# One wait each for the exponentials and the maxima, with eight fixed probability buffers

## The chip, the cores and the metric

The kernel runs on one core of one Trainium2 chip. The metric is device time in microseconds (us) of one execution, as the median of several runs. In the text PE is TensorE (matmuls; PEld are its weight loads), DVE is VectorE, ACT is ScalarE, POOL is GpSimd and SP is SyncE, which issues nearly all transfers. Each engine works through its own queue in order, and engines wait for each other by semaphores.

## The reference

Two attention blocks read the same input x of 2048 rows and 448 columns, with 16 heads of 28 columns each. Block A looks at eight keys per row (itself and every second row back), block B at all 2048. A gate per row mixes them:

```python
g = _sigmoid((x * gate_w).sum(-1, keepdims=True))
a = _A_ref(x, A_wqkv, A_wo)      # eight keys per row, dilation 2
b = _B_ref(x, B_wqkv, B_wo)      # full softmax attention
return g * a + (1 - g) * b

# inside _B_ref
scores = jnp.einsum("bhqd,bhkd->bhqk", q, k) * (Dh ** -0.5)
p = _softmax(scores, axis=-1)
o = jnp.einsum("bhqk,bhkd->bhqd", p, v)
```

## The kernel before

**Precision.** Float32 operands of the projections and the scores are split into a high part that the fast matmul format holds and a low part with the rest; three products (high with high, high with low, low with high) replace one.

**Stages.** From 0 to about 255 us the kernel projects x to q, k and v (lines 290 and 295), and computes the first row maxima on the side (lines 142 and 159). From about 255 to 840 us it runs the loop on which the change bears. After that come the last output projection and stores.

**The loop.** It has 16 units (a group of four heads by a block of 512 queries), each of 16 steps (128 keys), so 256 steps. In one step, `scores` issues on PE twelve score matmuls (line 955: four heads, three split products each), and between them up to three matmuls of another kind, s0, s1 and s2 (line 142): scores for the row maxima of a later unit. DVE reduces those to maxima (line 146), s0 alone and s1 with s2 as a pair. ACT takes the exponentials of the four heads as two instructions of two heads each (line 958). PE ends the step with eight matmul records that multiply the previous step's probabilities by V (line 921, called av). The maxima enter as two more rows of the contraction, so that the exponential needs no bias. In the last 20 steps all maxima are done, and s0 to s2 are left out.

**Its PSUM tiles.** Three tiles of two banks go round. One of them, called `one` in `scores` (T2 in the profile's buffer numbers), takes heads "1" and "2" in every step with s matmuls. The other two, `mine` and `other`, change places from step to step: `mine` takes heads "3" and "0", and `other` takes s1 and s2. So the pair of maxima that DVE takes from `other` must be done before PE may write head "3" of the next step there, and the second exponential of a step must be done before PE may write s1 and s2 of the next step. s0 has a bank of its own, T1.

**What sets the order.** The scheduling is by hand: each engine executes in the order of the code. A planner in the same file deals the work of block A (products on POOL, reductions on DVE, an exponential on ACT) to the steps. The semaphore waits are derived from the tiles that each instruction reads and writes. An instruction carries one wait itself; more waits become instructions of their own (EVENT_SEMAPHORE) ahead of it in the same queue.

**Probabilities.** Every exponential asks a pool of eight buffers for a new tile, `pair("P")`.

Of the kernel before, what the change touches and what calls it, by code (L numbers as in the profile page):

```python
# [10 lines left out]
AF = mybir.ActivationFunctionType  # L11
ALU = mybir.AluOpType
X = mybir.AxisListType.X
# [6 lines left out]
SCALE = DH ** -0.5  # L20
NU = NG * NB
NMX = 192
# [3 lines left out]
def gated_mix_kernel(ctx: ExitStack, tc: tile.TileContext, xT, xn, gw, wA, wB, woAB, out):  # L26
    nc = tc.nc
# [45 lines left out]
    MX = cp.tile([128, NMX], F32, name="MX")  # L73
# [10 lines left out]
    def pair(name):  # L84
        return pp.tile([128, 2, 512], F32, tag="P", name=name)
# [50 lines left out]
    def s1_mm(n, bank, half=False):  # L136
        u, i = divmod(n, 64)
        qs, kc, h = i // 16, i // 4 % 4, i % 4
        if i == 0 and u + 1 < NU:
            load_qhi(u + 1)  # L140
        r = slice(64 * (h // 2), 64 * (h // 2) + 64) if half else slice(32 * h, 32 * h + DH)
        nc.tensor.matmul(bank, qhis[u][h % 2][r, 128 * qs:128 * qs + 128],  # L142
                         KH[u // NB % 3][r, 512 * kc:512 * kc + 512], start=True, stop=True)

    def s1_max(n, k, bank):
        nc.vector.tensor_reduce(MX[:, n % NMX:n % NMX + k], bank, axis=X, op=ALU.max)  # L146
        if n // 64 != (n + k) // 64:
            finished.append(n // 64)
        s1c[0] = n + k
# [53 lines left out]
    with tc.tile_pool(name="xp", bufs=1) as xp, tc.tile_pool(name="wp", bufs=2) as wp:  # L203
# [208 lines left out]
        for kt in range(3):  # L412
            if kt < 2:
                nc.vector.tensor_copy(xh[0][:, kt, :], r[:, kt, :])
            nc.vector.tensor_tensor(out=xl[0][:, kt, :], in0=r[:, kt, :], in1=xh[0][:, kt, :].bitcast(F32),
                                    op=ALU.subtract)
        nc.vector.tensor_tensor(out=tail[64:128], in0=t[64:128], in1=tail[64:128].bitcast(F32), op=ALU.subtract)
        nc.vector.tensor_tensor(out=wl0[:, 3, 0:256], in0=wt0[:, 0:256], in1=wh0[:, 3, 0:256].bitcast(F32),
                                op=ALU.subtract)
# [27 lines left out]
        for n, t in enumerate(tiles):  # L447
# [4 lines left out]
            for w in splits:  # L452
                i, k = (n - splits[w][0]) * splits[w][1], splits[w][1]
# [42 lines left out]
            if n == 64:  # L496
                gate = []
                for sgn, dst in ((-1.0, g_t), (1.0, omg)):
                    e = sp.tile([128, NJ], F32, name="ez")
# [174 lines left out]
    for c in range(8):  # L674
# [20 lines left out]
        n = 0  # L695
# [236 lines left out]
    def scores(u, kt, cur):  # L932
        g = u // NB
        n = s1c[0]
        k = min(3, s1e - n)
        qh, ql = Qs[u]
        ks = slice(128 * kt, 128 * kt + 128)
        one, mine, other = ring
        ring[:] = (one, other, mine) if k else (other, one, mine)
        bank = {"1": one[:, 0, :], "2": one[:, 1, :], "3": mine[:, 0, :], "0": mine[:, 1, :],  # L940
                "s0": T1, "s1": other[:, 0, :], "s2": other[:, 1, :]}
        for tok in WITH if k else ALONE:
            if tok[0] == "s":
                i = int(tok[1])
                if i < k:
                    s1_mm(n + i, bank[tok])
                if i == 0:
                    s1_max(n, 1, T1)
                elif i == 2 and k > 1:
                    s1_max(n + 1, k - 1, other[:, 0:k - 1, :])  # L950
                continue
            a, t = tok[0], int(tok[1])
            h = (int(a) + n) % 4
            r = slice(32 * h, 32 * h + (DH + 2 if t == 0 else DH))
            nc.tensor.matmul(bank[a], (KH[g % 3], KH[g % 3], KL[g % 2])[t][r, ks], (qh, ql, qh)[t][r, :], start=(t == 0), stop=(t == 2))  # L955
            if t == 2 and a in "20":
                p = pair("P")
                nc.scalar.activation(p, one if a == "2" else mine, AF.Exp, scale=SCALE)  # L958
                cur[(h + 3) % 4], cur[h] = p[:, 0, :], p[:, 1, :]
                yield len(cur)  # L960

    for u in range(NU):
        g, b = divmod(u, NB)
        for kt in range(NJ):
# [12 lines left out]
            for a in scores(u, kt, cur):  # L977
                if a == 2:
                    run("mid", st)
# [66 lines left out]
```

## Time and profile before

| what | value |
|---|---|
| median of 3 runs | 921.59 us (920.6 to 921.7) |
| the profiled execution | 921.93 us |
| its span, first to last instruction | 920.1 us |
| busy: PE, DVE, ACT, POOL | 99%, 79%, 71%, 70% |
| granted clock of PE | 0.999 |
| from 255 to 800 us: DVE, ACT, POOL busy | 494, 478 and 484 of 545 us |

A profile's group of instructions is read as: line, engine, operation, what it writes and reads, shapes, count; then busy time in us and mean ns of one; then the idle time of the engine just before them and what ended it. In a timeline each row is a start in us, a duration in us, and the instruction; the time in brackets is the engine's idle time before it and what ended that. The chain of work lists, in order of time, what the end of the execution hung on; "issue" there is time in which nothing that the profile shows was waited for. An "ACTq" or "DVEq" belongs to the engine's queue, not to its arithmetic.

### The profile page before, as it was taken

How to read it: one execution, taken by the hardware profiler on the slowest of the kernel's cores; microseconds unless marked ns; L12 is line 12 of the kernel's file. 1: busy time of each engine (PE TensorE's matmuls, PEld its weight loads, DVE VectorE, ACT ScalarE, POOL GpSimd, SP SyncE). 2: the span in 40 equal slices, each digit the busy share in tenths (PEclk: the TensorE clock that was granted, in tenths of full speed). 3: DMA queues.
4: the chain of work that ended last, by engine and by line, in shares of the span. 5: the costliest groups of instructions: out<-in, count | busy, mean ns of one | idle time of the engine just before them, and what ended most of it. 6: DMA issues, size and time to landing. Idle time of an engine off the chain costs nothing.

```text
span 920.1 us, 21384 instructions
## 1 busy us (share of the span) xinstructions
PE 912.2 (99%) x8390; PEld 546.5 (59%) x8390; DVE 728.8 (79%) x934; ACT 650.0 (71%) x797; POOL 640.6 (70%) x505
## 2 busy tenths in 40 slices
PE   9999999999999999999999999999999999999998
PEld 6799999999944444444444444444444444335997
DVE  5588999998979999999999999999999988511221
ACT  6456434343388888888888888888888888996221
POOL 2489846464468649999899999999898996800100
PEclk9999999999999999999999999999999999999999
DMA  9877402558363341225235315421411322353772
GB/s 260 288 242 198 152 12 82 148 129 113 96 241 84 88 115 45 83 62 131 60 77 148 81 45 141 98 96 36 107 37 33 91 55 43 86 172 85 205 218 88
DMA packets 103966, 105.11 MB, mean 114 GB/s; under 512 B 64136, under 2 KB 73736, under 8 KB 103080
## 3 DMA queue, kind: packets, MB, share of 16 engines
q1 hardware_dynamic: 103720, 103.47, 41.3%
q8 instruction: 66, 1.08, 0.5%
q10 hardware_dynamic: 144, 0.26, 0.1%
q14 instruction: 36, 0.29, 0.1%
HBM read 62.72 MB, written 40.96 MB: 113 GB/s over the span
## 4 chain that ended last, share of the span: by engine, by line
PE 95%; DMA 3%; SPq 1%; ACT 1%; POOL 0%; DVE 0%; issue 0%; ACTq 0%
PE T L955 31%; PE av L921 28%; PE r L295 15%; PE T L804 7%; PE r L290 4%; PE r L142 4%; PE T L142 4%; DMA V<-in_xT 1%; DMA qk_hi<-qkh 1%; PE T L782 1%; DMA KH<-qk_hi 0%; SPq L217 0%; ACT P L958 0%; POOL wl L212 0%; DMA QP<-qk_hi 0%; ACT raw L358 0%
## 5 line engine op out<-in xcount | busy, mean ns | idle before, releaser
L958 ACT ACTIVATE P<-T 128x1024 f32<-128x1024 f32 x512 | 497.4, 1026 | 67.0 <-PE T L955 66.0
L146 DVE TENSOR_REDUCE MX<-T 128x1 f32<-128x512 f32 x470 | 448.9, 955 | 45.2 <-PE T L955 17.8
L921 PE MATMUL av<-P,V 128*32 128x512 f32 x2048 | 272.7, 605 | 0.9 <-ACT osb L822 0.9
L955 PEld LDWEIGHTS T<-QH,KH 30*128 30x128 f32 x1024 | 92.9, 181 | 238.3 <-ACT P L958 198.6
L142 PE MATMUL T<-KH,QP 28*128 28x512 f32 x704 | 225.0, 470 | 0.1
L955 PE MATMUL T<-QH,KH 30*128 30x512 f32 x1024 | 223.2, 493 | 0.2
L159 DVE TENSOR_REDUCE MX<-r 128x2 f32<-128x1024 f32 x160 | 192.1, 1222 | 25.6 <-PE r L142 22.3
L955 PE MATMUL T<-QL,KH 28*128 28x512 f32 x1024 | 191.9, 394 | 0.0
L955 PE MATMUL T<-QH,KL 28*128 28x512 f32 x1024 | 191.7, 391 | 0.0
L599 POOL TENSOR_TENSOR prod<-qt,kt 128x896 f32<-128x896 f32 x64 | 135.3, 2114 | 8.5 <-DMA kt<-a_scr 5.2
L358 ACT ACTIVATE raw<-r 128x896 f32<-128x896 f32 (+1 forms) x64 | 58.9, 921 | 97.9 <-PE r L295 94.6
L654 POOL TENSOR_TENSOR oat<-oat,prod 128x896 f32<-128x896 f32 x56 | 118.2, 2111 | 2.7
L142 PEld LDWEIGHTS T<-KH,QP 28*128 28x128 f32 x704 | 86.0, 181 | 24.7 <-ACT P L958 9.9
L359 POOL TENSOR_TENSOR ast<-raw 128x448 f32<-128x448 f32 x48 | 55.5, 1155 | 58.8 <-ACT raw L358 49.0
L649 POOL TENSOR_TENSOR prod<-vt,L 128x896 f32<-128x896 f32 x56 | 95.5, 1706 | 0.4
L955 PEld LDWEIGHTS T<-QH,KL 28*128 28x128 f32 x1024 | 93.6, 182 | 0.9
L955 PEld LDWEIGHTS T<-QL,KH 28*128 28x128 f32 x1024 | 93.6, 184 | 0.0
L921 PEld LDWEIGHTS av<-P,V 128*32 128x32 f32 x2048 | 40.3, 108 | 80.8 <-issue 67.6
L295 PE MATMUL r<-wh,xh 64*128 64x448 f32 (+1 forms) x512 | 82.9, 363 | 0.1
L142 PE MATMUL r<-KH,QP 64*128 64x512 f32 x320 | 80.6, 393 | 0.6 <-DVE MX L159 0.4
L295 PE MATMUL r<-wh,xl 64*128 64x448 f32 (+1 forms) x384 | 70.4, 364 | 0.0
L604 POOL TENSOR_TENSOR prod<-prod 128x448 f32<-128x448 f32 x64 | 65.6, 1026 | 5.0
(109 smaller groups left out, 1072.8 us busy)
## 6 DMA issues: line engine op xcount, KB each, us to landing
a_scr<-ast SPq DMA_DIRECT2D x24, 448.0 KB
qk_hi<-qkh SPq DMA_DIRECT2D x24, 256.0 KB
qk_lo<-qkh SPq DMA_DIRECT2D x24, 256.0 KB
rbc<-rs SPq DMA_DIRECT2D x64, 64.0 KB
QP<-qk_hi SPq DMA_DIRECT2D x64, 56.0 KB
KL<-qk_lo SPq DMA_DIRECT2D x16, 224.0 KB
QH<-qk_hi SPq DMA_DIRECT2D x64, 56.0 KB
QL<-qk_lo SPq DMA_DIRECT2D x64, 56.0 KB
```

The costliest lines, as they stand in the source:

```text
L142: nc.tensor.matmul(bank, qhis[u][h % 2][r, 128 * qs:128 * qs + 128], KH[u // NB % 3][r, 512 * kc:512 * kc + 512], start=True, stop=True)
L146: nc.vector.tensor_reduce(MX[:, n % NMX:n % NMX + k], bank, axis=X, op=ALU.max)
L159: nc.vector.tensor_reduce(m, PM[k], axis=X, op=ALU.max)
L295: nc.tensor.matmul(bank[:, 0:cols], x, ws[c][rows, k, 0:cols], start=first, stop=last)
L599: nc.gpsimd.tensor_tensor(out=p, in0=qt[c], in1=kvt["k", c % 2][:, HALO - DIL * w:HALO - DIL * w + NJ, :], op=ALU.mult)
L604: nc.gpsimd.tensor_tensor(out=lo, in0=lo, in1=hi, op=ALU.add)
L649: nc.gpsimd.tensor_tensor(out=dst.rearrange("p j (h d) -> p j h d", d=DH), in0=kvt["v", c % 2][:, HALO - DIL * w:HALO - DIL * w + NJ, :].r ...
L654: nc.gpsimd.tensor_tensor(out=oat[c], in0=oat[c], in1=oat[c, w], op=ALU.add)
L804: writes(bank, nc.tensor.matmul(bank[:, :D], src, wo[c][k], start=(first and k == ks[0] and i == 0), stop=(last and k == ks[-1] and i == 2)))
L921: nc.tensor.matmul(av[32 * h:32 * h + 32, :], V[:, kt, 4 * g + h, :], tiles_[h], start=(kt == 0), stop=(kt == NJ - 1), skip_group_check=True)
L955: nc.tensor.matmul(bank[a], (KH[g % 3], KH[g % 3], KL[g % 2])[t][r, ks], (qh, ql, qh)[t][r, :], start=(t == 0), stop=(t == 2))
L958: nc.scalar.activation(p, one if a == "2" else mine, AF.Exp, scale=SCALE)
```

## The change

The first eight exponentials take the eight buffers of the pool, and from then on each takes the buffer of the one eight before it, without asking the pool. Three kinds of dependence are declared absent: of an exponential on the exponential eight before it (both are ACT's, and PE's reading lies between), of an exponential on the last four pairs or singles of maxima, and of a maximum on the last eight exponentials. In each case the code's reason is that the wait for PE that stays behind implies the one that goes.

```diff
+    exps, maxs, probs = [], [], []
+
     def s1_max(n, k, bank):
-        nc.vector.tensor_reduce(MX[:, n % NMX:n % NMX + k], bank, axis=X, op=ALU.max)
+        i = nc.vector.tensor_reduce(MX[:, n % NMX:n % NMX + k], bank, axis=X, op=ALU.max)
+        for e in exps[-8:]:
+            tc.declare_no_dep(i.ins, e, reason="PE waited for it and the maximum waits for PE")
+        maxs.append(i.ins)
...
             if t == 2 and a in "20":
-                p = pair("P")
-                nc.scalar.activation(p, one if a == "2" else mine, AF.Exp, scale=SCALE)
+                if len(exps) < 8:
+                    probs.append(pair("P"))
+                p = probs[len(exps) % 8]
+                e = nc.scalar.activation(p, one if a == "2" else mine, AF.Exp, scale=SCALE).ins
+                for o in exps[-8:-7]:
+                    tc.declare_no_dep(e, o, query=mybir.DependencyQuery.ANY_SYNC,
+                                      reason="PE has read what it wrote, and this one waits for PE")
+                for o in maxs[-4:]:
+                    tc.declare_no_dep(e, o, reason="PE waited for it and the exponential waits for PE")
+                exps.append(e)
```

No instruction of arithmetic and no transfer changes its place on any engine. What changes is the list of waits. In ACT's queue the exponentials of the loop stood with two waits each; this is a stretch of the second unit before, behind the copy of the first unit's result (T_3270 is the tile `one`, the other two are `mine` in turn; PE_49, DVE_49, Activation_49 and DMAHW1_49 are the semaphores of PE, DVE, ACT itself and a transfer queue):

```order
L822 ACTIVATE osb<-av 128x512 [waits DMAHW1_49,PE_49]
L958 ACTIVATE P<-T_3270 128x1024 [waits PE_49,Activation_49]
L958 ACTIVATE P<-T_3266 128x1024 [waits DVE_49,PE_49]
L958 ACTIVATE P<-T_3270 128x1024 [waits PE_49,Activation_49]
L958 ACTIVATE P<-T_3262 128x1024 [waits DVE_49,PE_49]
```

The same stretch of ACT's queue with the change:

```order
L827 ACTIVATE osb<-av 128x512 [waits DMAHW1_49,PE_49,Activation_49]
L965 ACTIVATE P<-T_3270 128x1024 [waits PE_49]
L965 ACTIVATE P<-T_3266 128x1024 [waits PE_49]
L965 ACTIVATE P<-T_3270 128x1024 [waits PE_49]
L965 ACTIVATE P<-T_3262 128x1024 [waits PE_49]
```

In the whole program 277 exponentials lose a wait for ACT's own semaphore, which stood on the exponential itself while a separate instruction ahead held the wait for PE. Another 223 lose a wait for DVE, which was the separate instruction while the exponential held the wait for PE. 14 of the copies of line 822 (827 in the changed file) gain a wait for ACT's own semaphore, and their wait for PE moves to the separate instruction. ACT's queue has 197 instructions that only wait, against 694.

In DVE's queue the pairs of maxima (128x2) had two waits and the singles (128x1) one, here in the middle of the loop:

```order
L146 TENSOR_REDUCE MX<-T_3274 128x1 [waits PE_49]
L146 TENSOR_REDUCE MX<-T_3262 128x2 [waits PE_49,Activation_49]
L146 TENSOR_REDUCE MX<-T_3274 128x1 [waits PE_49]
L146 TENSOR_REDUCE MX<-T_3266 128x2 [waits PE_49,Activation_49]
L609 TENSOR_REDUCE L<-prod 128x16 [waits Pool_49]
```

The same place with the change:

```order
L148 TENSOR_REDUCE MX<-T_3274 128x1 [waits PE_49]
L148 TENSOR_REDUCE MX<-T_3262 128x2 [waits PE_49]
L148 TENSOR_REDUCE MX<-T_3274 128x1 [waits PE_49]
L148 TENSOR_REDUCE MX<-T_3266 128x2 [waits PE_49]
L614 TENSOR_REDUCE L<-prod 128x16 [waits Pool_49]
```

Here 233 pairs lose the wait for ACT, and with it the separate instruction that held the wait for PE. PE's, POOL's and SP's queues hold the same waits as before, for the same counts.

## Prediction

> **What bounds the kernel now.** The page comes first, for where time can be won at all, then the busy times of the three parts of the run.
>
> ```profile
> PE 912.2 (99%) x8390; PEld 546.5 (59%) x8390; DVE 728.8 (79%) x934; ACT 650.0 (71%) x797; POOL 640.6 (70%) x505
> ...
> 255.00:800.00 545.00, 544.67 (x5463) 224.09 (x5461) 494.18 (x676) 478.00 (x536) 483.88 (x344) 1.00 0.32 87
> 800.00:840.00 40.00, 39.09 (x371) 14.57 (x368) 5.29 (x10) 39.19 (x49) 4.07 (x4) 1.00 0.49 138
> 840.00:921.00 81.00, 76.28 (x403) 68.43 (x401) 16.13 (x39) 16.11 (x42) 2.80 (x3) 0.98 0.53 157
> ```
>
> The columns of the last three rows are stretch, length, then busy us and count of PE, PEld, DVE, ACT, POOL, then clock and DMA. PE looks full at 99%, but a matmul that has started and stands in a queue of others counts as busy, so this does not say that PE's own work sets the pace. The loop runs at the full clock and fills 545 + 40 us. No other engine is full up to 800 us (DVE 91%, POOL 89%, ACT 88%). Whatever the change does lies in the loop; the first 255 us and the last 81 us hold none of its instructions.
>
> So I read one pair of steps in the timeline, for what each start follows upon:
>
> ```profile
> 468.17 1.02 ACT L958 ACTIVATE P<-T 128x1024 f32<-128x1024 f32 x1
> 468.41 0.50 PE L955 MATMUL T<-QH,KH 30*128 30x512 f32 x2
> ...
> 469.24 0.18 PEld L142 LDWEIGHTS T<-KH,QP 28*128 28x128 f32 x2 [0.16 <-ACT P L958]
> 469.24 0.50 PE L142 MATMUL T<-KH,QP 28*128 28x512 f32 x2
> ...
> 469.48 1.94 ACT L958 ACTIVATE P<-T 128x1024 f32<-128x1024 f32 x2 [0.30 <-PE T L955]
> ...
> 469.85 1.22 DVE L146 TENSOR_REDUCE MX<-T 128x2 f32<-128x1024 f32 x1 [0.17 <-PE T L955]
> ...
> 470.68 0.19 PEld L955 LDWEIGHTS T<-QH,KH 30*128 30x128 f32 x2 [0.84 <-ACT P L958]
> ...
> 471.13 0.19 PEld L955 LDWEIGHTS T<-QH,KH 30*128 30x128 f32 x2 [0.15 <-DVE MX L146]
> ...
> 471.48 0.50 PE L142 MATMUL T<-KH,QP 28*128 28x512 f32 x2
> ...
> 473.02 0.50 PE L955 MATMUL T<-QH,KH 30*128 30x512 f32 x2
> ```
>
> Steps start at 468.41, 470.68 and 473.02. The pair of maxima of the first step starts at 469.85, 0.61 after its matmuls s1 and s2 (469.24). It ends at 471.07, and 0.06 later PE starts head "3" of the second step, which overwrites the tile of that pair. From there it is 1.89 us of PE's own work to the next step. The two steps add up without a remainder: 0.83 (step start to s2) + 0.61 + 1.22 + 0.06 + 1.89 = 4.61 us. This is a ring through DVE that takes two steps; what leaves it shortens a step by half as much.
>
> There is a second ring in it. s1 and s2 sat idle 0.16 us until the second exponential of the step before ended (468.17 + 1.02 = 469.19, and 0.05 later they start). That exponential follows the first one of its step without a pause: two take 1.94 us. So a first exponential that starts earlier frees s1 and s2 earlier, wherever they wait for ACT.
>
> The loop's waits, summed from 255 to 800 us (engine and line, whom for, total us, times, longest):
>
> ```profile
> PEld T L955 <- ACT P L958: 197.4, 236, 1.0
> ACT P L958 <- PE T L955: 65.2, 191, 0.6
> DVE MX L146 <- PE T L955: 17.8, 86, 0.5
> DVE MX L146 <- PE T L142: 10.8, 37, 1.9
> PEld T L142 <- ACT P L958: 9.9, 58, 0.4
> PEld av L921 <- ACT osb L822: 4.5, 14, 0.4
> ```
>
> The largest row misleads: the 0.84 us at 470.68 are time in which no weights are loaded while av runs. The first exponential of the step before, whose tile PE overwrites there, began at 469.48 and took 1.02, so it ended at 470.50, 0.18 us ahead of PE's step. A wait for ACT that really holds PE ends 0.05 us ahead (469.19 to 469.24). PE gains nothing from an earlier end there.
>
> **What a second wait costs.** The chain of work shows both kinds of start, in three places:
>
> ```profile
> 15.11 0.02 issue
> 15.12 0.02 ACTq L237
> 15.14 0.04 issue
> 15.19 0.63 ACT xh L237
> ...
> 476.59 0.02 issue
> 476.61 1.03 ACT P L958
> ...
> 42.88 0.02 issue
> 42.91 1.23 DVE MX L159
> ```
>
> With the wait as an instruction of its own (ACTq), ACT starts 0.08 us after the release; with the wait on the instruction itself, 0.02 us, and DVE also 0.02. Hence 0.06 us for each wait that ends in a separate instruction just ahead. That instruction's own record is short (its count, then its shortest, median and longest ns), and the pairs of maxima have idle time before them:
>
> ```profile
> L958 ACTq EVENT_SEMAPHORE  x506: 17/17/903, 255.7 to 838.7; - x169
> ...
> L146 DVE TENSOR_REDUCE MX<-T 128x2 f32<-128x1024 f32 x234 | 286.6, 1225 | 29.2 <-PE T L955 14.1 <-PE T L142 0.6
> ```
>
> The Trainium skill (Perfetto Trace Analysis, "Sequencer-only Instruction (DRAIN, etc)") says that such a record covers execution alone, while fetching and decoding what follows lie outside it. By the record of 0.017 us alone the maxima's term below would be 233 x 0.017 / 2 = 2.0 us; the row at 15.11 says 0.06, agrees with the page, and I go by it.
>
> **The terms.**
> - *233 pairs of maxima lose the separate wait.* No row of the chain shows such a start on DVE. Below, a price of nothing (if DVE prepares the next instruction under the one before); above, 0.61 - 0.50 = 0.11 less the 0.02 of a single wait, so 0.09. The nearest row is ACT's same arrangement, and I take 0.06. The pairs have the room: 29.2 us idle over 234 of them is 0.125 us each. In the ring of two steps: 233 x 0.06 / 2 = 7.0 us (0 to 10.5). Behind the pair on DVE stand block A's reductions and the next single; they start earlier with it, and nothing is queued that would hold it.
> - *277 exponentials lose their own wait behind the separate one.* These are mostly the first of a step. 191 of them waited for PE: 191 x 0.06 = 11.5 us come off ACT's idle time. On the path it counts only where s1 and s2 wait for ACT, and halved as it is the same ring. With the 58 listed waits it is 58 x 0.06 / 2 = 1.7 us, with all 191 it is 5.7 us. Waits under 0.1 us are not listed, so neither end is nearer: 3.7 us.
> - *223 exponentials lose the separate wait for DVE.* The separate instruction runs while the exponential before occupies ACT, and the wait for PE was already on the instruction itself. Nothing; without that cover it would be 0.06 each, of which the back-to-back 1.94 us shows no sign.
> - *The last 20 steps.* ACT is busy for 39.19 of 40 us, so at most 0.8 us is to be had; I take half, 0.4 us.
> - *14 copies gain a wait.* Their wait for PE moves to a separate instruction: 14 x 0.06 = 0.8 us lost, all of it on the path, as av waited for all 14.
> - *Eight fixed buffers.* The same eight turn as before, and no wait of PE changes. Nothing, with no cover needed.
>
> Sum: 7.0 + 3.7 + 0.4 - 0.8 = 10.3 us. The profiled execution took 921.93 us (1.8 us around its span of 920.1), so 911.6; it stands 0.3 us above the median of 921.59, which gives 911.3 us. What is late next is s1 and s2's place in PE's order, and after that the ring through ACT: the first exponential's tile is written again in the next step.
>
> **Rivals.**
> 1. *The separate wait on DVE is free.* The maxima's term goes, 3.3 us remain, 918.3 us. For it: no row prices the wait on DVE, and its record is as short as ACT's. Against it: the pair starts 0.11 us after the matmuls' recorded end, where a single wait takes 0.02. The Trainium skill (VectorE: DVE Perf Modes, "The DRAIN you can't avoid") reports that eight copies with a semaphore after each took as long as with one at the end, so that waits on DVE cost nothing there. By that rule this rival holds; no run here shows that case, where an instruction never waits for another engine.
> 2. *The whole 0.06 counts in each step.* If PE is held by head "3" so late that s1 and s2 follow it closely, the ring closes within one step: 233 x 0.06 + 3.3 = 17.3 us, 904.3 us. For it: in the second step above head "3" starts 0.45 us in. Against it: the s matmuls came 0.83 us after the step's start with ACT's wait and 0.80 without (470.68 to 471.48, in the same timeline), so PE's order sets them.
> 3. *PE's stream sets the pace.* 99% busy is then real, and the time stays at 921.6 us. Against it: the ring above closes only with the 0.11 us start of the maxima and the 0.06 of head "3" in it, and head "3" waits for DVE by the bracket at 471.13.
> 4. *Slower: block A on POOL falls behind.* Steps get shorter, POOL's work per step does not, and ACT's queue holds an instruction behind POOL's product:
>
> ```profile
> 361.92 1.30 POOL L851 TENSOR_TENSOR on<-osb,rbc 128x512 f32<-128x512 f32 x1
> ...
> 363.81 0.63 ACT L855 ACTIVATE onhi<-on 128x512 fp32r<-128x512 f32 x1
> ...
> L599 POOL TENSOR_TENSOR prod<-qt,kt 128x896 f32<-128x896 f32 x64 | 135.3, 2114 | 8.5 <-DMA kt<-a_scr 5.2
> ```
>
> Here the product ends at 363.22, 0.59 us before ACT needs it. If POOL loses more than this lead, ACT stops in front of the next exponentials. With one of POOL's 2.11 us products ahead of it in each of 14 units, that is 14 x (2.11 - 0.59) = 21.3 us lost against 10.3 gained: 932.6 us. It decides once POOL has no idle time left; 483.88 us of work in 545 - 10 = 535 us is 90%, so this is far.
>
> **How the numbers follow.** My forecast has a chance of 0.64, with a range of its own from 907 to 915. Rival 1 has 0.14, rival 2 0.10, rival 3 0.06, rival 4 0.06. The range takes in rivals 1 and 2 at their times, and the ends of the maxima's price: 904 to 918.5. A change of under 0.2%, 1.8 us, cannot be told from none. Rivals 3 and 4 fill the other two chances, and a fifth of rival 1 may fall within 0.2% as well: faster 0.85, same 0.09, slower 0.06.
>
> **What the changed profile would show.** The records of separate waits at the exponentials fall from 506 to a handful, and those at the maxima from 234 to one or two. The idle time of ACT before exponentials falls by some 11 us, that of DVE before the pairs from 29.2 us to about half. In a timeline the pair starts 0.55 instead of 0.61 us after s2, and the loop from 255 to 840 us ends near 830. If the pair still starts 0.6 us after s2, rival 1 is right; if it starts earlier and head "3" waits for something else, a wait has taken its place; if ACT's line 855 waits for POOL, it is rival 4.

## The result and the profile after

The changed kernel takes 911.37 us (median of 4 runs, 910.66 to 911.63) against 921.64 us for the kernel before (4 runs, 920.6 to 922.05): a ratio of 0.9889, 95% interval 0.9872 to 0.9906. That is 10.3 us less. 911.3 was forecast, but two of its terms were off in opposite directions, because the ring that carries both closes over three steps and not over two.

The profiled execution took 911.58 us. Its page, busy times first, then the two groups that the change touches (the changed file's line 965 was 958, line 148 was 146, 960 was 955, 926 was 921):

```profile
PE 901.1 (99%) x8390; PEld 547.1 (60%) x8390; DVE 731.8 (80%) x934; ACT 649.3 (71%) x797; POOL 640.0 (70%) x505
...
L965 ACT ACTIVATE P<-T 128x1024 f32<-128x1024 f32 x512 | 496.9, 1025 | 57.4 <-PE T L960 56.1
L148 DVE TENSOR_REDUCE MX<-T 128x1 f32<-128x512 f32 x470 | 448.4, 957 | 32.1 <-PE T L142 13.1
```

The work is the same: 497 and 449 us of exponentials and maxima before, 497 and 448 now. What shrank is the idle time in front of it, 67.0 to 57.4 us and 45.2 to 32.1 us. By shape, the idle time before the pairs of maxima went from 29.2 to 11.4 us:

```profile
L148 DVE TENSOR_REDUCE MX<-T 128x2 f32<-128x1024 f32 x234 | 286.7, 1225 | 11.4 <-PE T L960 1.7 <-PE T L142 0.3
```

The views of the two lines, after and then before, tell what happened to the separate waits, and how long the loop took (the last numbers of the rows of instructions are the first and the last start in us):

```profile
L965 ACT ACTIVATE P<-T x512: 1016/1024/1115, 255.5 to 828.2; 128x1024 f32<-128x1024 f32 x171
L965 ACTq EVENT_SEMAPHORE  x8: 17/28/904, 254.6 to 262.5; - x8
...
L148 DVE TENSOR_REDUCE MX<-T x470: 659/693/1229, 255.1 to 781.7; 128x1 f32<-128x512 f32 x79, 128x2 f32<-128x1024 f32 x78
L148 DVEq EVENT_SEMAPHORE  x1: 21/21/21, 256.1 to 256.1; - x1
```

```profile
L958 ACT ACTIVATE P<-T x512: 1017/1024/1127, 256.6 to 839.6; 128x1024 f32<-128x1024 f32 x171
...
L146 DVE TENSOR_REDUCE MX<-T x470: 627/697/1229, 256.1 to 792.7; 128x1 f32<-128x512 f32 x79, 128x2 f32<-128x1024 f32 x78
L146 DVEq EVENT_SEMAPHORE  x234: 21/21/21, 257.2 to 790.5; - x117
```

506 records of separate waits at the exponentials became 8, and 234 at the maxima became 1. From the first exponential to the last the loop takes 828.2 - 255.5 = 572.7 us, where it took 839.6 - 256.6 = 583.0: the whole gain of 10.3 us lies in it. From the last maximum to the last exponential, which spans the steps without s matmuls, it is 46.5 us against 46.9.

The timeline after shows one way through three steps (start, duration):

```profile
463.67 0.19 PEld L960 LDWEIGHTS T<-QH,KH 30*128 30x128 f32 x2 [0.84 <-ACT P L965]
...
464.68 1.94 ACT L965 ACTIVATE P<-T 128x1024 f32<-128x1024 f32 x2 [0.22 <-PE T L960]
...
466.53 1.91 DVE L148 TENSOR_REDUCE MX<-T 128x1 f32<-128x512 f32 x2
466.67 0.18 PEld L142 LDWEIGHTS T<-KH,QP 28*128 28x128 f32 x2
...
468.49 0.18 PEld L960 LDWEIGHTS T<-QH,KH 30*128 30x128 f32 x2
...
470.38 0.19 PEld L960 LDWEIGHTS T<-QH,KH 30*128 30x128 f32 x2 [0.84 <-ACT P L965]
```

A step starts at 463.67, and its first exponential 1.01 us later; before, that was 1.07 (468.41 to 469.48). The second exponential ends at 464.68 + 1.94 = 466.62, and s1 and s2 of the next step start 0.05 later. DVE's row holds the single and the pair and ends at 468.44; the pair takes 1.23 of it, so it starts at 467.21, 0.54 us after s1 and s2, where it was 0.61. Head "3" of the step after that starts 0.05 after the pair's end, and 1.89 us later, at 470.38, the step behind that one begins.

The kernel before goes the same way. The prediction's rows show the exponentials from 469.48 to 471.42 and s1 and s2 at 471.48; the next rows of that timeline are the single and the pair, and head "3" behind them:

```profile
471.28 2.03 DVE L146 TENSOR_REDUCE MX<-T 128x1 f32<-128x512 f32 x2
...
473.37 0.18 PEld L955 LDWEIGHTS T<-QH,KH 30*128 30x128 f32 x2
```

So s1 and s2 at 471.48 wait for ACT no less than those at 469.24, which the prediction took for the case with ACT's wait. No wait is listed for them, because the weight loads had been idle for 0.05 us only: the list leaves out idle times up to 0.15 us (and not 0.1, as the prediction has it).

That such starts add up to the time of three steps shows nothing yet, for the pieces of any path from one start to another do. A link that binds is known by its time being the same in every step, and by the step changing with it, which the experiments below test. The table has the middle value, and in brackets the range without the lowest and the highest tenth, of 228 of the 234 steps with pairs of maxima, computed from the starts in the two traces; a step starts with its first weight load.

| link, us | before | changed |
|---|---|---|
| step's start to its first exponential | 1.073 (1.066 to 1.094) | 1.012 (1.005 to 1.023) |
| its start to the second one's end | 1.941 (1.939 to 1.944) | 1.941 (1.939 to 1.943) |
| to s1 of the next step | 0.051 (0.050 to 0.051) | 0.051 (0.050 to 0.051) |
| to the pair's start | 0.612 (0.607 to 0.617) | 0.543 (0.537 to 0.562) |
| to the pair's end | 1.225 (1.223 to 1.226) | 1.225 (1.224 to 1.226) |
| to head "3" of the step after | 0.053 (0.052 to 0.053) | 0.054 (0.053 to 0.054) |
| to the start of the step behind that | 1.894 (1.887 to 1.904) | 1.898 (1.888 to 1.920) |
| a third of their sum | 2.283 | 2.241 |
| a third of three steps, measured | 2.283 | 2.242 |
| for comparison: step's start to s1 | 0.784 (0.718 to 0.860) | 0.735 (0.707 to 0.855) |

The seven links form one ring through PE, ACT and DVE that closes over three steps. Two of them changed, each by the wait that went: 0.061 us on ACT and 0.069 on DVE. What leaves any one of them shortens a step by a third. From a step's start to s1, which the prediction's ring of two steps had as 0.83 us of PE's order, the time varies by 0.14 us: that is no link of the ring.

The listed waits from 255 to 840 us do not show this. Those of the s weights for ACT rose:

```profile
PEld T L142 <- ACT P L965: 22.0, 123, 0.2
```

They were 9.9 us in 58 waits before, and the waits of head "3" for the maxima (PEld T L960 for L148, before L955 for L146) fell from 50 to 1. Yet in both kernels s1 starts within 0.075 us of the second exponential's end, and head "3" within 0.075 us of the pair's end, in at least 232 of the 234 steps.

### The profile page after: what moved, and what is told of

The parts are those of the page before. It is cut to its first block, busy times and chain, and to the rows that moved or that the text cites. A ratio compares the mean times of both kernels' runs of the same rounds, so it can differ in the third digit from the quotient of the medians.

```text
span 909.8 us, 20654 instructions
## 1 busy us (share of the span) xinstructions
PE 901.1 (99%) x8390; PEld 547.1 (60%) x8390; DVE 731.8 (80%) x934; ACT 649.3 (71%) x797; POOL 640.0 (70%) x505
## 4 chain that ended last, share of the span: by engine, by line
PE 95%; DMA 2%; ACT 2%; DVE 1%; issue 0%; SPq 0%; ACTq 0%; DVEq 0%
PE T L960 29%; PE av L926 27%; PE r L300 15%; PE r L295 7%; PE T L809 6%; PE T L142 5%; PE r L142 4%; DMA oal<-oa_scr 1%; ACT P L965 1%; PE T L787 1%; DMA V<-in_xT 1%; DMA KH<-qk_hi 0%; ACT KH L748 0%; DVE res L818 0%; DVE xl L420 0%
## 5 line engine op out<-in xcount | busy, mean ns | idle before, releaser
L965 ACT ACTIVATE P<-T 128x1024 f32<-128x1024 f32 x512 | 496.9, 1025 | 57.4 <-PE T L960 56.1
L148 DVE TENSOR_REDUCE MX<-T 128x1 f32<-128x512 f32 x470 | 448.4, 957 | 32.1 <-PE T L142 13.1
L960 PEld LDWEIGHTS T<-QH,KH 30*128 30x128 f32 x1024 | 92.7, 181 | 228.9 <-ACT P L965 197.8
L142 PE MATMUL T<-KH,QP 28*128 28x512 f32 x704 | 221.4, 460 | 0.1
L960 PE MATMUL T<-QH,KH 30*128 30x512 f32 x1024 | 212.0, 489 | 0.5 <-DMA QH<-nm 0.5
L960 PE MATMUL T<-QH,KL 28*128 28x512 f32 x1024 | 186.7, 394 | 0.0
L960 PE MATMUL T<-QL,KH 28*128 28x512 f32 x1024 | 185.4, 393 | 0.0
L960 PEld LDWEIGHTS T<-QH,KL 28*128 28x128 f32 x1024 | 93.5, 183 | 0.7
L960 PEld LDWEIGHTS T<-QL,KH 28*128 28x128 f32 x1024 | 93.6, 184 | 0.0
```

The source lines that it names most:

```text
L148: i = nc.vector.tensor_reduce(MX[:, n % NMX:n % NMX + k], bank, axis=X, op=ALU.max)
L965: e = nc.scalar.activation(p, one if a == "2" else mine, AF.Exp, scale=SCALE).ins
```

## The experiments

Ratios are to the kernel before on the same chip, and a gain in us is (1 - ratio) x 921.6. "Loop" is the time from the start of the first exponential to that of the last, in the profiled execution, and "step" the middle value of a third of three steps there.

| kernel | ratio (95% interval) | loop us | step us | s weights' wait for ACT, us and times | idle before pairs us |
|---|---|---|---|---|---|
| before | 1 | 583.0 | 2.283 | 9.9, 58 | 29.2 |
| changed | 0.9889 (0.9872 to 0.9906) | 572.7 | 2.242 | 22.0, 123 | 11.4 |
| maxima only | 0.9945 (0.993 to 0.996) | 577.9 | 2.261 | 21.4, 114 | 18.2 |
| exponentials only | 0.994 (0.9923 to 0.9956) | 578.5 | 2.265 | 2.1, 13 | 22.1 |
| exponentials' own waits only | 0.9953 (0.9938 to 0.9968) | 578.0 | 2.265 | 1.9, 12 | 21.9 |
| before, shorter pairs | 0.9946 (0.9931 to 0.9961) | 578.2 | 2.262 | 22.6, 122 | 34.4 |
| changed, copies' wait gone | 0.9886 (0.9871 to 0.9901) | 572.8 | 2.242 | 22.0, 124 | 11.4 |
| changed, shorter pairs | 0.985 (0.9835 to 0.9864) | 568.6 | 2.220 | 37.6, 202 | 14.8 |
| changed, second exponential 480 | 0.9862 (0.9845 to 0.9878) | 569.6 | 2.225 | 3.3, 20 | 5.2 |
| changed, both shorter | 0.9808 (0.9793 to 0.9822) | 564.9 | 2.202 | 23.4, 131 | 7.2 |
| changed, second exponential 448 | 0.9826 (0.981 to 0.9843) | 566.2 | 2.210 | none | 0.9 |
| the same, maxima with two waits | 0.9899 (0.9884 to 0.9914) | 573.3 | 2.244 | none | 11.2 |

The four kernels with shorter exponentials leave out probabilities, and the two with shorter pairs alone leave keys out of the maxima; they are there for their times.

### Each half alone

The maxima's half alone is the changed file without the exponentials' edits:

```diff
-                if len(exps) < 8:
-                    probs.append(pair("P"))
-                p = probs[len(exps) % 8]
+                p = pair("P")
...
-                for o in exps[-8:-7]:
-                    tc.declare_no_dep(e, o, query=mybir.DependencyQuery.ANY_SYNC, ...)
-                for o in maxs[-4:]:
-                    tc.declare_no_dep(e, o, ...)
```

> The kernel before, in which only the maxima lose their wait for ACT; the exponentials keep the pool's buffers and their waits (109 of the second exponentials of a step get a wait for ACT's own semaphore in place of what the maxima brought them, behind an exponential that covers it). Two-step ring through DVE: 233 x 0.06 / 2 = 7.0 us less than before, ratio 0.992, about 914.6 us, with the pair of maxima starting about 0.06 us earlier after s2. If the separate wait on DVE is free (rival 1): 921.6 us, ratio 1.000. If the whole 0.06 counts in each step (rival 2): 233 x 0.06 = 14.0 us less, ratio 0.985.

The exponentials' half alone is the changed file without the maxima's edit:

```diff
-        for e in exps[-8:]:
-            tc.declare_no_dep(i.ins, e, ...)
```

> The changed kernel, in which only the maxima keep their two waits. Theory: the exponentials' term alone, 3.7 + 0.4 - 0.8 = 3.3 us less than before, 918.3 us, ratio 0.996. If rival 1 is right, this part holds the whole measured gain: 911.4 us, ratio 0.989. If the exponentials do not reach the path: 921.6 + 0.8 for the copies' new wait, ratio 1.001.

Measured: 5.1 us for the maxima (0.0055 x 921.6) and 5.5 us for the exponentials. Together 10.6, against 10.2 for both at once by their ratio: the halves add up. The wait on DVE is not free (rival 1, which had 921.6 us for the maxima alone), and it does not count in full in each step (rival 2, 14.0 us). But the maxima brought 5.1 us and not 7.0, the exponentials 5.5 and not 3.3; 7.0 lies outside the first interval (3.7 to 6.5 us), 3.3 below the second (4.1 to 7.1).

Each half changed one link of the ring and left the other six within 0.004 us of the kernel before. With the maxima's half the pair starts 0.543 us after s1 instead of 0.612, and a step is 0.022 us shorter; with the exponentials' half the first exponential starts 1.013 us into the step instead of 1.073, and a step is 0.018 us shorter. Both are about a third of what the link lost. Over 233 steps a third makes 233 x 0.069 / 3 = 5.4 us and 233 x 0.060 / 3 = 4.7 us; the loops are 5.1 and 4.5 us shorter.

The listed waits look as if ACT had taken something back from the maxima. First the maxima alone, then the exponentials alone:

```profile
PEld T L142 <- ACT P L963: 21.4, 114, 0.4
```

```profile
PEld T L142 <- ACT P L963: 2.1, 13, 0.2
```

But s1 starts within 0.075 us of the second exponential's end in at least 232 of the 234 steps in both kernels, as before. What the list counts is how long the weight loads had been idle by then, when that is over 0.15 us.

### Time of the same size elsewhere in the ring

If the ring through DVE is real, a pair of maxima that is shorter by about the cost of the wait must bring as much as the missing wait.

```diff
     def s1_max(n, k, bank):
-        nc.vector.tensor_reduce(MX[:, n % NMX:n % NMX + k], bank, axis=X, op=ALU.max)
+        c = 480 if k == 2 else 512
+        nc.vector.tensor_reduce(MX[:, n % NMX:n % NMX + k], bank[..., 0:c], axis=X, op=ALU.max)
```

> The kernel before with all its waits, in which each pair of maxima reads 480 of the 512 keys of each matmul (32 keys per matmul are left out of the maxima). By the profile a pair of 1024 elements takes 1225 ns and a single of 512 takes 688, so 64 fewer elements are 64 x 537 / 512 = 67 ns, about what the removed wait was priced at. Two-step ring: 234 x 0.067 / 2 = 7.9 us less, 913.8 us, ratio 0.991, though no wait is touched. One-step ring: 15.7 us less, ratio 0.983. PE's stream sets the pace: ratio 1.000.

```profile
L147 DVE TENSOR_REDUCE MX<-T 128x2 f32<-128x960 f32 x234 | 271.0, 1158 | 34.4 <-PE T L956 16.8 <-PE T L142 1.1
```

The pair takes 1158 ns instead of 1225, so 67 ns less. All waits are in place, and the result is that of the maxima's half: ratio 0.9946 against 0.9945, loop 578.2 against 577.9 us. The wait counts as time in the ring, no differently from arithmetic. Here too the forecast of a half, 7.9 us, fails: 5.0 us came, and a third of 234 x 0.067 is 5.2.

### The exponentials' waits for DVE

This kernel has the eight fixed buffers and the edit on the exponential eight before, but keeps the 223 separate waits for DVE and all waits of the maxima.

```diff
-                for o in maxs[-4:]:
-                    tc.declare_no_dep(e, o, ...)
```

> The kernel before, with the eight fixed buffers and without the 277 waits of exponentials for ACT's own semaphore; the 223 separate waits for DVE and all waits of the maxima stay. If a separate wait that runs under the exponential before it costs nothing, this is as fast as the version with all of the exponentials' part (916.5 us, ratio 0.994). If those 223 cost what the others do, some 2.4 us of that part's 5.4 us are missing: 918.9 us, ratio 0.997.

```profile
L963 ACT ACTIVATE P<-T x512: 1017/1024/1097, 258.1 to 836.1; 128x1024 f32<-128x1024 f32 x171
L963 ACTq EVENT_SEMAPHORE  x229: 17/17/903, 257.1 to 789.3; - x115
```

The ratios of the two kernels (0.9953 and 0.994) have intervals that overlap and do not decide it. The traces do: with 229 records of separate waits or with 8 the two exponentials of a step take 1.94 us together, and a step takes 2.265 us. These waits cost nothing there. Their records begin about 1 us before the exponential ahead of them ends. The gain on ACT is that of the waits which stood between PE's release and the exponential.

### The copies that gained a wait

```diff
-        t = mp.tile([128, 512], F32, name="osb")
-        nc.scalar.activation(t, av, AF.Copy)
-        fin["o"] = t
+        if "o" not in fin:
+            fin["o"] = mp.tile([128, 512], F32, name="osb")
+        i = nc.scalar.activation(fin["o"], av, AF.Copy).ins
+        if "c" in fin:
+            tc.declare_no_dep(i, fin["c"], query=mybir.DependencyQuery.ANY_SYNC, ...)
+        fin["c"] = i
```

> The changed kernel with one fixed buffer for the copy of av and without the wait that 14 of these copies had gained. By the sum of the prediction 14 x 0.06 = 0.8 us less than the changed kernel, 910.6 us, ratio to before 0.988. If the copies' new wait is hidden: the same 911.4 us as the changed kernel.

The loop is 572.8 us against 572.7, and the ratio 0.9886 against 0.9889. No gain shows. It does not quite settle the term: without the copy's wait for ACT, other short copies on ACT got waits (the trace has ten separate ones at line 181 that the changed kernel's does not have).

### With ACT out of the way

The next two kernels take ACT out of the ring. Their second exponential of a step reads 448 of 512 queries per head; one has the maxima's single wait, the other their two.

```diff
+                    if len(probs) % 2 == 0:
+                        nc.gpsimd.memset(probs[-1][:, :, 448:512], 0.0)
...
-                e = nc.scalar.activation(p, one if a == "2" else mine, AF.Exp, scale=SCALE).ins
+                c = 512 if a == "2" or not k else 448
+                e = nc.scalar.activation(p[:, :, 0:c], (one if a == "2" else mine)[:, :, 0:c], AF.Exp, scale=SCALE).ins
```

> The changed kernel, in which the second exponential of a step takes 448 of 512 queries per head (the other probabilities of those heads are left out), about 106 ns less, so that s1 and s2 should not wait for ACT any more. It is the counterpart of the next one. Theory: hardly faster than with 480 queries (ratio 0.985 to 0.986), since nothing on ACT is waited for there; ACT's waits of the s weights under 3 us.

> The same shortened exponentials with the two waits of the maxima restored. If ACT took back the missing part of the maxima's term, the maxima's wait is now worth its full half, 233 x 0.06 / 2 = 7.0 us to 8.2 us (at 0.07): ratio 0.993 to 0.994, and the loop (first to last exponential) 7.0 to 8.2 us longer than with 448 queries and no second wait. If the ring gives a third of the wait whatever ACT does, the difference is again 5 us: ratio 0.991.

The second one, by shape and by first and last start, and then the first:

```profile
L966 ACT ACTIVATE P<-T x512: 909/1024/1105, 257.7 to 831.0; 128x1024 f32<-128x1024 f32 x93, 128x896 f32<-128x896 f32 x78
...
L148 DVE TENSOR_REDUCE MX<-T 128x2 f32<-128x1024 f32 x234 | 286.7, 1225 | 11.2 <-PE T L958 0.9
```

```profile
L968 ACT ACTIVATE P<-T x512: 910/1024/1105, 257.0 to 823.2; 128x1024 f32<-128x1024 f32 x93, 128x896 f32<-128x896 f32 x78
...
L148 DVE TENSOR_REDUCE MX<-T 128x2 f32<-128x1024 f32 x234 | 286.6, 1225 | 0.9 <-PE T L960 0.4 <-PE T L142 0.2
```

The same edit of the maxima is now worth 573.3 - 566.2 = 7.1 us of the loop, and 913.17 - 906.0 = 7.2 us of the whole (ratios 0.9899 and 0.9826, intervals apart). That is half of 233 x 0.06, but it does not mean that ACT had taken back 2 us in the kernel before: here another ring binds. The pair no longer starts a fixed time after s1 (0.613 to 0.719 us with two waits, 0.540 to 0.591 with one), but it does after the step's start: 1.315 us (1.306 to 1.327) and 1.248 us (1.239 to 1.265). From there it is the pair, head "3" and the next start but one: (1.315 + 1.225 + 0.053 + 1.894) / 2 = 2.244 us and (1.248 + 1.225 + 0.053 + 1.894) / 2 = 2.210 us, which are the measured steps. This is the prediction's ring of two steps, in which 0.067 us count by half. What sets the pair's start at 1.25 us is open: with one wait it follows the single on DVE without a pause, but PE's order of the s matmuls could set the same time.

One expectation failed: 448 queries were to be hardly faster than 480. They brought another 3.4 us of the loop (569.6 to 566.2). At 480 the listed waits for ACT were down to 3.3 us, but s1 still started within 0.075 us of the second exponential's end in at least 230 of the 234 steps. That exponential was still a link of the ring of three steps, which gave way to the ring of two only on the way to 448.

### What bounds the changed kernel

The same two shortenings on the changed kernel, each alone and together.

```diff
-        i = nc.vector.tensor_reduce(MX[:, n % NMX:n % NMX + k], bank, axis=X, op=ALU.max)
+        i = nc.vector.tensor_reduce(MX[:, n % NMX:n % NMX + k], bank[..., 0:480 if k == 2 else 512], axis=X, op=ALU.max)
```

> The changed kernel, in which each pair of maxima reads 480 of 512 keys of each matmul (32 keys per matmul are left out of the maxima), 67 ns less. The same 67 ns gave 5.0 us on the kernel before. The ring through DVE still binds, but s1 and s2 already wait for ACT in 123 steps: 4 to 5 us less than the changed kernel, 906.4 to 907.4 us, ratio to before 0.983 to 0.984, with more than 22 us of waits of the s weights for ACT. If nothing but DVE's ring counted: 7.9 us less, 903.5 us, ratio 0.980. If ACT already caps the loop: 911.4 us, ratio 0.989.

> The changed kernel, in which the second exponential of each step with s matmuls takes 480 of 512 queries per head (the others' probabilities are left out for those heads; four buffers are cleared once for it), about 0.83 ns x 64 = 53 ns less by the rows of 896 and 1024 elements (920 and 1026 ns). If s1 and s2's waits for the second exponential are what took half of the maxima's gain: 123 x 0.053 / 2 = 3.3 us less than the changed kernel, 908.1 us, ratio 0.985, and the waits of the s weights for ACT fall from 22 us to a few. If these waits lie beside the path: 911.4 us, ratio 0.989.

> Both shortenings on the changed kernel, with both parts left out. If DVE's ring was held back by ACT, the pair's 67 ns now bring their full half or near it: 3.3 + 7.9 = 11.2 us less than the changed kernel at most, 900 to 903 us, ratio 0.977 to 0.980. If the two only add what they bring alone: 903 to 904 us. If PE's own order limits next: no faster than the better of the two.

```profile
PEld T L142 <- ACT P L965: 37.6, 202, 0.3
```

That is the changed kernel with shorter pairs: 202 of 234 pairs of s matmuls now have a listed wait for ACT. A step is 0.022 us shorter than the changed kernel's, a third of the 0.067 that the pair lost. With the shorter second exponential alone it is 0.017 us shorter, a third of 0.054 (the two exponentials take 1.887 us instead of 1.941). With both it is 0.040 us shorter, a third of 0.121. The loops are 4.1, 3.1 and 7.8 us shorter; in the last two the first step is some 1 us longer (5.8 us instead of 4.9), while POOL clears the buffers. So the changed kernel is still bound by the one ring of three steps, in which DVE's pair and ACT's exponentials count alike. The 11.2 us that two rings of two steps would have given did not come, and the expectation that the exponential acts by the 123 listed waits came near its time for another reason.

The kernel with shorter pairs has the lowest ratio, 0.985, of those that compute all probabilities. A softmax does not depend on the number that is subtracted, so its output is still the softmax; but its guard against overflow sees 480 of 512 keys in each of the paired matmuls.

## Why the prediction was right, and where it was off

- **That the time came out was luck**: the maxima's term was 1.9 us too large and the exponentials' 1.2 to 2.2 us too small (7.0 and 3.3 us forecast; 5.1 and 4.5 to 5.5 measured). Right were the prices of the two waits, that both lie on a ring through PE, and that neither counts in full in each step.
- **The step that failed: the ring of two steps.** The prediction took the time from a step's start to s2 (0.83 and 0.80 us) as PE's own, and only the first of the two as a wait for ACT. By its own rows the second follows ACT as well: 469.48 + 1.94 = 471.42, and s2 starts at 471.48. That its pieces added up to 4.61 us without a remainder proved nothing. The runs showed one ring over three steps, with ACT's two exponentials and DVE's pair in it, in which the change of any one link counts by a third. The ring of two steps binds only where the second exponential is cut to 448 queries.
- **Mis-sized: the maxima's term.** 7.0 us was a half of 233 x 0.06; a third of 233 x 0.069 is 5.4, and 5.1 came.
- **Mis-sized: the exponentials' term.** The prediction weighed it by the waits that a list shows, halved, and took 3.7 us between 1.7 and 5.7; with 0.4 from the last steps and less 0.8 for the copies that made 3.3. A third of 233 x 0.060 is 4.7; measured are 5.5 us by the ratio and 4.5 by the loop.
- **The price of 0.06 us on DVE**, taken from ACT's row, was near: the pair starts 0.069 us earlier after s1. The Trainium skill's rule (VectorE: DVE Perf Modes, "The DRAIN you can't avoid", semaphores that cost nothing between copies) does not carry over to a wait for another engine: 5.1 us came from 233 of them.
- **Rival 2** did not come, but the reason given against it, that PE's order sets s1 and s2, does not hold: they followed ACT in both steps.
- **The last 20 steps**: 0.4 us forecast, 0.4 measured (46.9 to 46.5 us).
- **The copies**: 0.8 us lost was forecast. av's listed waits for the copies were 5.8 us in 15 before and 6.2 in 15 after, and removing the wait showed no gain. Not settled.
- **The 223 waits under a running exponential** cost nothing, as forecast.
- **Rival 4** did not come: POOL is busy for 484 us from 255 to 800 us as before, and ACT's line 860 does not wait for it in any listed wait.

## What to carry to other kernels

A second semaphore wait is not a detail of bookkeeping when the instruction is next on a ring: on this kernel each costs 0.06 to 0.07 us if its release ends the engine's idle time, and cost nothing on ACT where it passed some 1 us before the engine was free. To size its removal, find the ring and count over how many steps it closes. A path whose pieces add up to the time of a step is not yet the ring: look at each link in many steps, and keep those whose time hardly varies. Do not go by a list of waits for this. Here a listed wait of 197 us (the weight loads at a step's start) held nothing, and a link that bound in every step was listed in 58 of 234.

## What the runs showed of the hardware

The separate wait has a record of only 17 ns on ACT and 21 on DVE, but costs more from release to start: on ACT 0.08 us with it and 0.02 without, on DVE 0.07 us of the pair's start after s1. On DVE the pair starts 43 to 44 ns after the end of that record. PE's weight loads start 0.05 us after the recorded end of the exponential or the pair that they wait for. And it made no difference whether 67 ns of the ring were arithmetic or waiting: 5.0 us from shorter pairs, 5.1 from fewer waits.
